# A gated recurrence with a gated convolution behind it: inputs loaded in pieces of 128 tokens, small weights on another queue, four gate tiles in flight

## The chip, the cores and the metric

The kernel runs on one core of a Trainium2 chip. A core has five engines that work side by side and wait for one another through semaphores: TensorE (PE in the profile, its weight loads PEld), VectorE (DVE), ScalarE (ACT), GpSimd (POOL) and SyncE (SP), which here only issues transfers. Sixteen DMA engines move data between HBM and the core's memory. The metric is the device time of one execution in microseconds, the median of several runs.

## The reference

The inputs are `x`, `r_gate` and `i_gate`, each 4 x 6336 x 256 in float32, 25,344 tokens of 256 features in all. Cut to what matters:

```python
log_a = 8.0 * sigmoid(r_gate) * np.log(np.clip(sigmoid(a_param), 1e-6, 1 - 1e-6))
a_t   = np.exp(log_a)
x_g   = np.sqrt(np.maximum(1 - a_t * a_t, 1e-6)) * sigmoid(i_gate) * x
for t in range(S):
    h = a_t[:, t] * h + x_g[:, t]          # a recurrence along the sequence
    y[:, t] = h
gate = sigmoid(causal_conv(y, conv_w))     # five taps, each feature by itself
out  = (gate * (y @ w_val)) @ w_out        # both 256 x 256
```

Every input element is read once and every output element written once: 104 MB with the output.

## The kernel before

**Tiles.** The tokens are cut into 51 tiles `g`, 48 of 512 tokens and three of 256, and these into 28 chunks `c`, mostly of two tiles (`CHUNKS`). Loading, the gates and the output work by tile; the recurrence works by chunk and by half `h` of the 256 features; the square root works by unit, a group of one to three chunks (`UNITS`), because ScalarE needs another function table for it than for exp and tanh.

**One tile's way.** `load` brings `r` and `i` into a buffer `ri` (`NIN` = 3 of them); `r` puts four consecutive tokens on each partition (L248), `i` puts token j x 128 + p on partition p (L249). `loadx` brings `x` in the same way as `i` (L255, `NX` = 5 buffers). `tanh` (L343, ScalarE) makes both gates' tanh in one instruction. `u2` forms (tanh + 1) * x, on VectorE in one instruction (L350) or on GpSimd in two (L353 and L354); the string `U2` says which for each tile. `srT` turns the r half with TensorE so that features lie on partitions (L327), `exp` makes a (L366, ScalarE), `e` squares it (L374, GpSimd), `sq` takes the root (L378, ScalarE, by unit), `nT` turns that back (L387) and `xg` multiplies it into `u` (L394, VectorE). `xT` turns `u` (L327), `scan` runs the recurrence (L415, VectorE), `conv` does the five taps as matmuls with diagonal weights (L441), `tg` is the gate's tanh (L449, ScalarE), `val` and `out` are the two products (L457, L479), `gv` joins gate and value (L467, VectorE), `osb` moves the result out of PSUM (VectorE at L490 or ScalarE at L492, by the string `OSB`), and `store` writes a tile (L497, `NOSB` = 3 buffers).

**Order.** All of it is written out by a planner. `make_jobs` lists each operation's engine, an assumed cost from `COST` and what it depends on; the buffer counts are such dependencies, for instance a load of tile g on the tanh of tile g - `NIN`:

```python
job("load", "DMA", f, [("tanh", g - NIN)])
```

`make_plan` then simulates the engines greedily, the earliest start first and `PRIO` where starts tie, and the kernel emits the operations in the order of the planned starts. Each engine runs its instructions in that order, whatever the chip's real times are. So another cost, priority or string moves instructions on all engines. Every load and store is issued by SyncE, in order: an issue that waits holds back all transfers behind it. The framework gives the transfers eight completion semaphores in turn, so that a transfer also waits until the one eight places before it has landed.

**Setup.** `ap2` (L260) and `wrow` (L262) are small parameters at the head of SyncE's queue; the first six planned loads follow. ScalarE makes log(sigmoid(`a_param`)) by a tanh (L289) and an Ln (L296). The two matrices are cast on their way by GpSimd's own queue.

Of the kernel before, what the change touches and what calls it, by code (L numbers as in the profile page):

```python
# [9 lines left out]
P = 128  # L10
# [5 lines left out]

CHUNKS = [[256], [512]] + [[512, 512]] * 23 + [[512], [256], [256]]

UNITS = [2, 2, 1, 3, 3, 3, 3, 3, 2, 2, 1, 3]
NS = 10  # L20
NE = 8
NU = 10
NY = 6
NIN = 3
NX = 5
NTR = 3
NTI = 6
# [2 lines left out]
BANKS = 4  # L30
PB = dict(srT=2, nT=2, xT=2, ops=2)

OSB = ("DDDDDDDDDADDDDDDDDDDDADDADDDDDDDDADDDADDDDDADADADDDDDDDDDDADADDDDDDAAADDADDDAADADAAADADDAA"
       "AAAADDAAA")

U2 = "PDPDDDDPPPPDDDPPDPPDPPPPPPPPPPPPPPPPDPPPPPPPPPDPPPP"

COST = dict(load=(0.1, 2.7), loadx=(0.05, 1.45), tanh=(0.2, 1.7), u2P=(0.25, 3.15), u2D=(0.15, 1.07), srT=(0.05, 0.45), exp=(0.35, 0.86), e=(0.1, 1.8),
            sq=(0.3, 1.71), nT=(0.05, 0.47), xg=(0.1, 0.58), xT=(0.05, 0.45), scan=(0.21, 2.14), conv=(0.2, 1.1), tg=(0.19, 0.83),
            val=(0.02, 0.93), gv=(0.15, 1.07), out=(0.02, 0.47), osbD=(0.68, 0), osbA=(0.59, 0),  # L40
            store=(0.1, 1.2))
PRIO = dict(load=-0.26, loadx=5.59, store=-2, tanh=6, exp=3.87, sq=5.27, tg=-0.62, srT=-2, nT=2.67, xT=-2,
            conv=4.33, val=-0.49, out=3.64, e=4.3, u2=5.81, xg=1.63, scan=5.49, gv=3.24, osb=-2)
TABLE, SEM, DMA_LAT = 1.3, 0.15, 2.2
FP32 = mybir.dt.float32
BF16 = mybir.dt.bfloat16
ACT = mybir.ActivationFunctionType
ALU = mybir.AluOpType


class Shape:
# [3 lines left out]
    def __init__(self, total, seq):  # L55
# [15 lines left out]
        self.runs, self.npos, batch_of = [], [], []  # L71
        for u, n in enumerate(UNITS):
            runs = []
# [35 lines left out]
def make_jobs(sh):  # L109

    jobs = {op: [] for op in PRIO}
    unit_of = [u for u, n in enumerate(UNITS) for _ in range(n)]
    ends = [sum(UNITS[:u + 1]) for u in range(len(UNITS))]
    qlast = [max(q for q, (w, _) in enumerate(sh.pieces) if w == g) for g in range(len(sh.tiles))]

    def job(op, eng, f, deps, cost=None, bank=0):
        fix, per = COST[cost or op]
        jobs[op].append((eng, fix + per * f, [d for d in deps if d[1] >= 0], bank))  # L120

    for g, (_, n) in enumerate(sh.tiles):
        f = n / WIN
        c = sh.chunk_of[g]
        job("load", "DMA", f, [("tanh", g - NIN)])
        job("loadx", "DMA", f, [("u2", g - NX)])
        job("tanh", "ACT", f, [("load", g), ("u2", g - NTI)]
            + ([("srT", 2 * sh.chunk_of[g - NTR] + 1)] if g >= NTR else []))
        job("u2", "DVE" if U2[g] == "D" else "POOL", f, [("tanh", g), ("loadx", g)] + ([("xT", 2 * sh.chunk_of[g - NU] + 1)] if g >= NU else []), "u2" + U2[g])
        job("nT", "PE", f, [("sq", unit_of[c]), ("xg", g - PB["nT"])], None, 1)  # L130
# [18 lines left out]
    for q, (g, i) in enumerate(sh.pieces):  # L149
        job("out", "PE", 1, [("gv", g), ("osb", q - PB["ops"])], None, 1)  # L150
        job("osb", "DVE" if OSB[q] == "D" else "ACT", 1, [("out", q), ("store", g - NOSB)], "osb" + OSB[q])
    for u, n in enumerate(UNITS):
        size = sum(sh.chunks[c][1] for c in range(ends[u] - n, ends[u])) / CHUNK
        fix, per = COST["sq"]
        jobs["sq"].append(("ACT", fix * len(sh.runs[u]) + per * size, [("e", 2 * ends[u] - 1)], 0))
# [3 lines left out]
def make_plan(sh):  # L159

    jobs = make_jobs(sh)
    reads = dict(exp="srT", xg="nT", scan="xT", osb="out")
    nxt = dict.fromkeys(jobs, 0)
    done, free, order, mode = {}, {}, [], "E"
    bank_free, banks = [0.0] * BANKS, {}
    while True:
        best = None
        for op, todo in jobs.items():  # L170
            i = nxt[op]
            if i == len(todo):
                continue
            eng, dur, deps, need = todo[i]
            t = free.get(eng, 0.0)
            if need:
                b = min(bank_free)
                if b == math.inf:
                    continue
                if b:  # L180
                    t = max(t, b + SEM)
            for d in deps:
                e = done.get(d)
                if e is None:
                    break
                if e + SEM > t:
                    t = e + SEM
            else:
                if best is None or (t, PRIO[op]) < best[:2]:
                    best = (t, PRIO[op], op, i, eng, dur, need)  # L190
        if best is None:
            break
        t, _, op, i, eng, dur, need = best
        if eng == "ACT" and op != "osb":
            if (op == "sq") != (mode == "S"):
                dur += TABLE
            mode = "S" if op == "sq" else "E"
        free[eng] = t + dur
        done[op, i] = t + dur + (DMA_LAT if eng == "DMA" else 0.0)
        if need:  # L200
            banks[op, i] = bank_free.index(min(bank_free))
            bank_free[banks[op, i]] = math.inf
        if op in reads:
            bank_free[banks[reads[op], i]] = t + dur
        order.append((t, op, i, eng, dur))
        nxt[op] += 1
    assert all(nxt[op] == len(todo) for op, todo in jobs.items()), nxt
    order.sort(key=lambda o: o[0])
    return order, banks
# [3 lines left out]
def kernel(  # L213
# [11 lines left out]
    nc = tc.nc  # L225
    B, S, D = x.shape
    assert D == 2 * P, f"kernel assumes D == 256, got {D}"
    H = D // P

    xf = x.rearrange("b s d -> (b s) d")  # L230
    rf = r_gate.rearrange("b s d -> (b s) d")
    if_ = i_gate.rearrange("b s d -> (b s) d")
# [6 lines left out]
    const = ctx.enter_context(tc.tile_pool(name="const", bufs=1))  # L239
# [3 lines left out]
    def load(g):  # L243
        t0, nt = tiles[g]
        nj = nt // P
        ri = inp.tile([P, 2, SUB, D], FP32, name="ri", tag="ri", bufs=NIN)

        nc.sync.dma_start(ri[:, 0, 0:nj, :], rf[t0:t0 + nt, :].rearrange("(p j) d -> p j d", j=nj))  # L248
        nc.sync.dma_start(ri[:, 1, 0:nj, :], if_[t0:t0 + nt, :].rearrange("(j p) d -> p j d", p=P))  # L249
        live["ri", g] = ri  # L250

    def loadx(g):
        t0, nt = tiles[g]
        xt = inp.tile([P, SUB, D], FP32, name="xt", tag="xt", bufs=NX)
        nc.sync.dma_start(xt[:, 0:nt // P, :], xf[t0:t0 + nt, :].rearrange("(j p) d -> p j d", p=P))  # L255
        live["xt", g] = xt

    with tc.manual_schedule():
        ap2 = const.tile([H, P], FP32, name="ap2")
        nc.sync.dma_start(ap2[:], a_param.rearrange("(h p) -> h p", p=P))  # L260
        wrow = const.tile([CONV_K, D], FP32, name="wrow")
        nc.sync.dma_start(wrow[:], moe_conv_w[:, :])  # L262
        before = [(op, g) for _, op, g, eng, _ in plan if eng == "DMA"][:6]
        for op, g in before:
            (load if op == "load" else loadx)(g)

        ident_f = const.tile([P, P], FP32, name="ident_f")
        make_identity(nc, ident_f[:])
# [16 lines left out]
        with tc.tile_pool(name="ps_setup", bufs=1, space=bass.MemoryType.PSUM) as ps_setup:  # L285
            kps = ps_setup.tile([P, H], FP32, name="kps")
            nc.tensor.transpose(out=kps[:], in_=ap2[0:H, :], identity=ident_f[0:H, 0:H])
            kt = const.tile([P, H], FP32, name="kt")
            nc.scalar.activation(out=kt[:], in_=kps[:], func=ACT.Tanh, scale=0.5)  # L289
            ksig = const.tile([P, H], FP32, name="ksig")  # L290
            nc.vector.tensor_scalar(out=ksig[:], in0=kt[:], scalar1=0.5, scalar2=0.5,
                                    op0=ALU.mult, op1=ALU.add)
            nc.vector.tensor_scalar(out=ksig[:], in0=ksig[:], scalar1=1e-6, scalar2=1.0 - 1e-6,
                                    op0=ALU.max, op1=ALU.min)
            kln = const.tile([P, H], FP32, name="kln")
            nc.scalar.activation(out=kln[:], in_=ksig[:], func=ACT.Ln)  # L296
            nc.vector.tensor_scalar(out=khf[:], in0=kln[:], scalar1=0.5 * C_SCALE, scalar2=None, op0=ALU.mult)
            wc_ps = ps_setup.tile([P, H, CONV_K], FP32, name="wc_ps")
            for h in range(H):
                nc.tensor.transpose(out=wc_ps[:, h, :], in_=wrow[0:CONV_K, h * P:(h + 1) * P],  # L300
                                    identity=ident_f[0:CONV_K, 0:CONV_K])
            nc.vector.tensor_copy(out=wcol[:], in_=wc_ps[:])
        diag = const.tile([P, H, CONV_K, P], BF16, name="diag")
        for h in range(H):
            for kk in range(CONV_K):
                nc.vector.tensor_scalar(out=diag[:, h, kk, :], in0=ident_f[:], scalar1=wcol[:, h, kk:kk + 1],
                                        scalar2=None, op0=ALU.mult)
# [186 lines left out]
        def op_store(g, eng):  # L494
# [6 lines left out]
                           nT=op_nT, xg=op_xg, xT=op_xT, scan=op_scan, conv=op_conv, tg=op_tg, val=op_val, gv=op_gv,  # L501
                           out=op_out, osb=op_osb, store=op_store)
# [32 lines left out]
```

## Time and profile before

| | |
|---|---|
| time, median of 3 runs (lowest to highest) | 323.8 us (321.44 to 326.42) |
| span of the profiled run | 324.1 us |
| busy: ScalarE | 289.5 us, 89% |
| busy: VectorE | 270.2 us, 83% |
| busy: TensorE, its weight loads | 246.5 us, 76%; 161.6 us, 50% |
| busy: GpSimd | 236.1 us, 73% |
| moved by DMA | 104.56 MB, mean 323 GB/s |
| packets of SyncE's queue | 67,022, 90.1% of 16 engines' span |
| granted TensorE clock, mean | 0.967 |

Busy time counts instructions that compute; waits, semaphore instructions and the issuing of transfers are not in it. A table by stage gives for each stretch of the span its length and, engine by engine, the busy microseconds with the number of instructions, then the TensorE clock, the DMA engines' busy share and the rate. The share can pass 1 because an engine's packets overlap. A line of waits reads: who waited for whom, microseconds in total, number of waits, the longest. A line of a transfer's issues reads: kind, count, size of one, median microseconds from issue to landing.

### The profile page before, as it was taken

To read this page: it belongs to the slowest core of one execution; us is meant where nothing else is said; L and a number is where in the kernel's file an instruction comes from. 1 tells how busy PE (TensorE), PEld (TensorE's weight loads), DVE (VectorE), ACT (ScalarE), POOL (GpSimd) and SP (SyncE) were. 2 spreads that over 40 slices of the span, in tenths; PEclk is the share of its full clock that TensorE was granted. 3 is DMA by queue.
4 is the path that set the end of the run, shared out by engine and by line. 5 is a ranking of instruction groups with operands and counts; after the bars stand their busy time and mean duration, and the time that the engine had idled before them with its cause. 6 is when DMAs were issued, how large, how long until landed. Compare 5 with 4: busy or idle time off the path is not lost.

```text
span 324.1 us, 7354 instructions
## 1 busy us (share of the span) xinstructions
PE 246.5 (76%) x2987; PEld 161.6 (50%) x2987; DVE 270.2 (83%) x265; ACT 289.5 (89%) x230; POOL 236.1 (73%) x146
## 2 busy tenths in 40 slices
PE   1148426796687787797988778797779896989994
PEld 0044325454455455564654465464546654655653
DVE  3126649999899699999999679988987997999993
ACT  6898899899886899999998999799969999899953
POOL 6427552999899759996599999999995790299200
PEclk9999769999999799999999999999989997999999
DMA  7999999999999999999999999999999984323344
GB/s 217 349 363 375 330 338 357 363 316 389 342 368 385 381 306 342 355 389 400 381 337 404 392 381 310 401 387 395 374 389 377 344 280 169 131 101 161 131 197 194
DMA packets 68432, 104.56 MB, mean 323 GB/s; under 512 B 4391, under 2 KB 55342, under 8 KB 68398
## 3 DMA queue, kind: packets, MB, share of 16 engines
q1 hardware_dynamic: 67022, 103.83, 90.1%
q0 software_dynamic: 1376, 0.26, 0.9%
q8 instruction: 23, 0.38, 0.5%
q14 instruction: 11, 0.09, 0.1%
HBM read 78.39 MB, written 25.95 MB: 322 GB/s over the span
## 4 chain that ended last, share of the span: by engine, by line
ACT 20%; DVE 18%; PE 18%; DMA 17%; issue 14%; POOL 10%; SPq 2%; ACTq 0%; DVEq 0%; POOLq 0%
DMA ri<-in_i_gate_dram 10%; DVE yring L415 9%; DMA xt<-in_x_dram 7%; ACT tring L343 6%; PE bank L479 5%; ACT ering L378 4%; POOL ering L374 4%; PE gp L441 4%; POOL uring L354 4%; PE val L457 3%; ACT tg L449 3%; PE bank L327 3%; DVE gv L467 3%; DVE osb L490 3%; DVE uring L394 3%
## 5 line engine op out<-in xcount | busy, mean ns | idle before, releaser
L374 POOL TENSOR_TENSOR ering<-aring 128x1024 f32<-128x1024 f32 (+2 forms) x56 | 97.5, 1765 | 44.6 <-ACT aring L366 36.5
L415 DVE TENSOR_TENSOR_SCAN yring<-aring,yring,bank 128x1024 bf16<-128x1024 f32 (+5 forms) x54 | 109.4, 2046 | 0.4 <-PE bank L327 0.4
L354 POOL TENSOR_TENSOR uring<-t,xt 128x1024 bf16<-128x1024 f32 (+1 forms) x39 | 89.9, 2304 | 18.2 <-DMA xt<-in_x_dram 9.1
L343 ACT ACTIVATE tring<-ri 128x2048 bf16<-128x2048 f32 (+1 forms) x51 | 93.9, 1865 | 10.0 <-DMA ri<-in_i_gate_dram 9.6
L441 PE MATMUL gp<-yring,diag 64*64 64x512 bf16 (+16 forms) x1196 | 68.2, 351 | 8.6 <-ACT tg L449 6.4
L479 PE MATMUL bank<-wo,gv 128*128 128x256 bf16 x396 | 58.1, 279 | 10.5 <-DVE gv L467 3.7
L467 DVE SCALAR_TENSOR_TENSOR gv<-tg,val 128x1024 bf16<-128x1024 bf16 (+1 forms) x54 | 60.3, 1120 | 6.7 <-PE val L457 4.3
L366 ACT ACTIVATE aring<-bank,khf 128x1024 f32<-128x1024 bf16 (+2 forms) x56 | 59.4, 1109 | 6.2 <-PE bank L327 5.6
L449 ACT ACTIVATE tg<-gp 128x1024 bf16<-128x1024 f32 (+1 forms) x51 | 51.1, 1002 | 6.5 <-PE gp L441 6.4
L457 PE MATMUL val<-yring,wv 128*128 128x512 bf16 (+1 forms) x204 | 52.8, 383 | 4.1 <-DVE gv L467 3.9
L490 DVE COPY osb<-bank 128x512 f32<-128x512 f32 x69 | 45.6, 679 | 8.6 <-PE bank L479 7.4
L479 PEld LDWEIGHTS <-gv 128*128 128x128 bf16 x396 | 36.7, 99 | 29.4 <-issue 14.6
L378 ACT ACTIVATE ering<-ering,b 128x2048 bf16<-128x2048 f32 (+3 forms) x15 | 46.7, 3112 | 2.3 <-POOL ering L374 1.9
L441 PEld LDWEIGHTS <-diag 64*64 64x64 bf16 x1196 | 31.6, 108 | 32.6 <-issue 17.4
L387 PE MATMUL bank<-ident_b,ering 128*128 128x128 bf16 x396 | 30.7, 231 | 22.2 <-ACT ering L378 19.8
L353 POOL TENSOR_SCALAR t<-tring 128x1024 f32<-128x1024 bf16 (+1 forms) x39 | 45.0, 1154 | 2.0
L394 DVE TENSOR_TENSOR uring<-bank,uring 128x1024 bf16<-128x1024 bf16 (+1 forms) x51 | 33.0, 666 | 15.9 <-PE bank L387 9.6
L327 PE MATMUL bank<-ident_b,tring 128*128 128x128 bf16 x396 | 32.1, 232 | 17.3 <-ACT tring L343 12.5
L387 PEld LDWEIGHTS <-ering 128*128 128x128 bf16 x396 | 26.0, 104 | 27.9 <-ACT ering L378 22.8
L327 PEld LDWEIGHTS <-tring 128*128 128x128 bf16 x396 | 26.0, 104 | 25.9 <-ACT tring L343 14.2
L327 PE MATMUL bank<-ident_b,uring 128*128 128x128 bf16 x396 | 31.9, 224 | 8.9 <-DVE uring L394 6.0
L327 PEld LDWEIGHTS <-uring 128*128 128x128 bf16 x396 | 25.4, 101 | 17.4 <-DVE uring L394 8.0
(31 smaller groups left out, 109.2 us busy)
## 6 DMA issues: line engine op xcount, KB each, us to landing
ri<-in_r_gate_dram SPq DMA_DIRECT2D x48, 512.0 KB, 7.0
ri<-in_i_gate_dram SPq DMA_DIRECT2D x48, 512.0 KB, 7.9
xt<-in_x_dram SPq DMA_DIRECT2D x48, 512.0 KB, 8.0
out_dram<-osb SPq DMA_DIRECT2D x48, 512.0 KB, 4.9
ri<-in_r_gate_dram SPq DMA_DIRECT2D x3, 256.0 KB, 3.2
ri<-in_i_gate_dram SPq DMA_DIRECT2D x3, 256.0 KB, 3.4
xt<-in_x_dram SPq DMA_DIRECT2D x3, 256.0 KB, 7.5
out_dram<-osb SPq DMA_DIRECT2D x3, 256.0 KB, 2.0
```

Of the source, the lines that this page charges most:

```text
L327: nc.tensor.transpose(out=dst[:, col:col + P], in_=src[:, j, h * P:(h + 1) * P], identity=ident_b[:])
L343: nc.scalar.activation(out=tring[:, r:i + 1:i - r, 0:nj, :], in_=ri[:, :, 0:nj, :], func=ACT.Tanh, scale=0.5)
L354: nc.gpsimd.tensor_tensor(out=u, in0=t1, in1=xt, op=ALU.mult)
L366: nc.scalar.activation(out=aring[:, h, a0:a0 + nt].rearrange("c (w p j) -> c w p j", p=P, j=nj), in_=live.pop(("srT", k))[:, 0:nt].rearran ...
L374: nc.gpsimd.tensor_tensor(out=ering[:, h, e0:e0 + nt], in0=a, in1=a, op=ALU.mult)
L378: nc.scalar.activation(out=nring[:, :, 2 * e0:2 * e0 + m], in_=ering[:, :, e0:e0 + m], func=ACT.Sqrt, scale=-0.25, bias=b025[:, 0:1])
L415: nc.vector.tensor_tensor_scan(out=yring[:, h, y0 + c0:y0 + c1], data0=aring[:, h, a0 + c0:a0 + c1], data1=xT[:, c0:c1], initial=0.0 if fr ...
L441: nc.tensor.matmul(out=gp[64 * h:64 * h + 64, m, c0:c1], lhsT=diag[rows, h, kk, rows], rhs=yring[rows, h, src:src + c1 - c0], start=(sh == 0),
L449: nc.scalar.activation(out=tg[:, :, 0:nt], in_=live.pop(("gp", g))[:, :, 0:nt], func=ACT.Tanh, scale=0.5)
L457: nc.tensor.matmul(out=val[:, m, 0:nt], lhsT=wv[:, hk, m * P:(m + 1) * P], rhs=yring[:, hk, y0:y0 + nt], start=(hk == 0), stop=(hk == H - 1))
L467: nc.vector.scalar_tensor_tensor(out=gv[:, 0:nj, hs, :].rearrange("c j h p -> c j (h p)"), in0=tg[:, hs, 0:nt].rearrange("c h (p j) -> c j ...
L479: nc.tensor.matmul(out=ops[:, e * D:(e + 1) * D], lhsT=gv[:, 2 * i + e, hk, :], rhs=wo[:, hk, :], start=(hk == 0), stop=(hk == H - 1))
```

## The change

It has four parts. First, the loads of `i` and `x` are split: one transfer per 128 tokens instead of one per tile. Such a transfer reads 128 rows of 1 KB that lie in a row in HBM, one to each partition[...]. Second, the two small parameters go on ScalarE's queue, and ScalarE's start uses exp and Ln, which share a function table, with the tanh table loaded by an instruction of its own that waits for nothing. Third, four instead of three buffers for the gates. Fourth, the planner starts DMA and ScalarE at a later planned time (`START`, `ACT_START`), costs `u2` on VectorE higher, and has new priorities, units and strings: 13 units for 12; `u2` on VectorE for 7 tiles for 12; `osb` on VectorE for 69 pieces as before, in other places.

```diff
-UNITS = [2, 2, 1, 3, 3, 3, 3, 3, 2, 2, 1, 3]
+UNITS = [1, 1, 2, 1, 2, 4, 3, 3, 3, 3, 1, 2, 2]
-NIN = 3
+NIN = 4
-U2 = "PDPDDDDPPPPDDDPPDPPDPPPPPPPPPPPPPPPPDPPPPPPPPPDPPPP"
+U2 = "DPPPDPPPPPDDPPPDDPPPPPPPPPPPPPPPPPPPPPPDPPPPPPPPPPP"
...
-PRIO = dict(load=-0.26, loadx=5.59, store=-2, tanh=6, exp=3.87, sq=5.27, tg=-0.62, srT=-2, nT=2.67, xT=-2,
-            conv=4.33, val=-0.49, out=3.64, e=4.3, u2=5.81, xg=1.63, scan=5.49, gv=3.24, osb=-2)
+PRIO = dict(load=3.81, loadx=4.34, store=2.61, tanh=1.36, exp=-1.22, sq=0.49, tg=-1.74, srT=-1.43, nT=0.13,
+            xT=2.16, conv=3.97, val=0.26, out=1.67, e=4.3, u2=6, xg=-2, scan=4.12, gv=-1.47, osb=-2)
+START, ACT_START = 0.9, 4.6
...
-    done, free, order, mode = {}, {}, [], "E"
+    done, free, order, mode = {}, dict(DMA=START, ACT=ACT_START), [], "E"
...
-        nc.sync.dma_start(ri[:, 1, 0:nj, :], if_[t0:t0 + nt, :].rearrange("(j p) d -> p j d", p=P))
+        for j in range(nj):
+            nc.sync.dma_start(ri[:, 1, j, :], if_[t0 + j * P:t0 + (j + 1) * P, :])
...
-        nc.sync.dma_start(xt[:, 0:nt // P, :], xf[t0:t0 + nt, :].rearrange("(j p) d -> p j d", p=P))
+        for j in range(nt // P):
+            nc.sync.dma_start(xt[:, j, :], xf[t0 + j * P:t0 + (j + 1) * P, :])
...
-        nc.sync.dma_start(ap2[:], a_param.rearrange("(h p) -> h p", p=P))
+        nc.scalar.dma_start(ap2[:], a_param.rearrange("(h p) -> h p", p=P))
-        nc.sync.dma_start(wrow[:], moe_conv_w[:, :])
+        nc.scalar.dma_start(wrow[:], moe_conv_w[:, :])
+        nc.scalar.preload_act_table_set("natural_log_exp_and_others")
...
-            nc.scalar.activation(out=kt[:], in_=kps[:], func=ACT.Tanh, scale=0.5)
+            nc.scalar.activation(out=kexp[:], in_=kps[:], func=ACT.Exp, scale=-1.0)
-            nc.vector.tensor_scalar(out=ksig[:], in0=kt[:], scalar1=0.5, scalar2=0.5,
-                                    op0=ALU.mult, op1=ALU.add)
+            nc.vector.tensor_scalar(out=ksig[:], in0=kexp[:], scalar1=1.0, scalar2=None, op0=ALU.add)
+            nc.vector.reciprocal(out=ksig[:], in_=ksig[:])
...
             nc.scalar.activation(out=kln[:], in_=ksig[:], func=ACT.Ln)
+            nc.scalar.preload_act_table(ACT.Tanh)
```

More of the change, by code (lines that the diff above doesn't have):

```diff
@@ L31 @@
 PB = dict(srT=2, nT=2, xT=2, ops=2)
-OSB = ("DDDDDDDDDADDDDDDDDDDDADDADDDDDDDDADDDADDDDDADADADDDDDDDDDDADADDDDDDAAADDADDDAADADAAADADDAA"
+OSB = ("DDDDDDDDDDDDDDADDDDDDDDADDDDDDDDDDDDDDDDDDDDDDDDDADDDAAADAADADDDDDAAADADAADADDDAAAADAAADDD"
        "AAAADDAAA")
-U2 = "PDPDDDDPPPPDDDPPDPPDPPPPPPPPPPPPPPPPDPPPPPPPPPDPPPP"
-COST = dict(load=(0.1, 2.7), loadx=(0.05, 1.45), tanh=(0.2, 1.7), u2P=(0.25, 3.15), u2D=(0.15, 1.07), srT=(0.05, 0.45), exp=(0.35, 0.86), e=(0.1, 1.8),
+U2 = "DPPPDPPPPPDDPPPDDPPPPPPPPPPPPPPPPPPPPPPDPPPPPPPPPPP"
+COST = dict(load=(0.1, 2.7), loadx=(0.05, 1.45), tanh=(0.2, 1.7), u2P=(0.25, 3.15), u2D=(0.2, 1.55), srT=(0.05, 0.45), exp=(0.35, 0.86), e=(0.1, 1.8),
             sq=(0.3, 1.71), nT=(0.05, 0.47), xg=(0.1, 0.58), xT=(0.05, 0.45), scan=(0.21, 2.14), conv=(0.2, 1.1), tg=(0.19, 0.83),
@@ L287 @@
             nc.tensor.transpose(out=kps[:], in_=ap2[0:H, :], identity=ident_f[0:H, 0:H])
-            kt = const.tile([P, H], FP32, name="kt")
-            nc.scalar.activation(out=kt[:], in_=kps[:], func=ACT.Tanh, scale=0.5)
+            kexp = const.tile([P, H], FP32, name="kexp")
+            nc.scalar.activation(out=kexp[:], in_=kps[:], func=ACT.Exp, scale=-1.0)
             ksig = const.tile([P, H], FP32, name="ksig")
-            nc.vector.tensor_scalar(out=ksig[:], in0=kt[:], scalar1=0.5, scalar2=0.5,
-                                    op0=ALU.mult, op1=ALU.add)
+            nc.vector.tensor_scalar(out=ksig[:], in0=kexp[:], scalar1=1.0, scalar2=None, op0=ALU.add)
+            nc.vector.reciprocal(out=ksig[:], in_=ksig[:])
             nc.vector.tensor_scalar(out=ksig[:], in0=ksig[:], scalar1=1e-6, scalar2=1.0 - 1e-6,
```

## The prediction

> **What bounds the kernel now.** I read the table of stages first (busy time of each engine in each stretch of the span, then TensorE clock, DMA share, GB/s), because the page's mean shares (ScalarE 89%, VectorE 83%, DMA about 90%) mix a start, a stream and a drain.
>
> ```profile
> 0.00:10.00 10.00, 1.22 (x7) 0.81 (x7) 3.22 (x16) 6.53 (x9) 6.16 (x14) 1.00 0.86 237
> 10.00:20.00 10.00, 2.46 (x20) 1.97 (x20) 1.11 (x1) 9.24 (x8) 2.67 (x3) 1.00 1.11 362
> 80.00:120.00 40.00, 30.95 (x381) 20.14 (x382) 35.69 (x35) 33.93 (x26) 32.92 (x17) 0.96 1.01 357
> 200.00:240.00 40.00, 32.01 (x384) 20.96 (x381) 37.37 (x34) 35.74 (x27) 38.25 (x22) 1.00 1.06 384
> 280.00:300.00 20.00, 18.37 (x236) 11.02 (x235) 20.00 (x15) 19.09 (x24) 17.90 (x14) 1.00 0.29 115
> 300.00:324.00 24.00, 20.04 (x240) 12.40 (x236) 18.21 (x24) 15.31 (x19) 1.62 (x3) 0.98 0.44 176
> ```
>
> After PE and its weight loads come VectorE, ScalarE, GpSimd. From 10 to about 260 us the DMA engines are full (share 1.01 to 1.11, 352 to 384 GB/s, 367 as the mean of 40 to 240 us) and ScalarE is about 92% busy; from 280 us there are only stores, and VectorE and ScalarE are full. So two resources stand level: the queue of transfers, and ScalarE with 289.5 us of work. ScalarE idles 34.6 us in all: 3.5 before 10 us, 8.7 after 300 us, some 22 between. The waits say for what:
>
> ```profile
> ACT tring L343 <- DMA ri<-in_i_gate_dram: 9.6, 9, 2.2
> POOL uring L354 <- DMA xt<-in_x_dram: 9.1, 4, 4.3
> ACT tg L449 <- PE gp L441: 6.4, 9, 1.3
> DVE uring L350 <- DMA xt<-in_x_dram: 6.2, 4, 2.6
> ACT aring L366 <- PE bank L327: 5.6, 7, 1.3
> ```
>
> (total, times, longest). ScalarE waits for gate tiles 9.6 us, the largest entry that more gate buffers can touch; x makes GpSimd and VectorE wait 15.3 us. Then the queue of SyncE, its own waits and issues (min/median/max ns of one issue):
>
> ```profile
> SPq L497 <- DVE osb L490: 91.6, 38, 5.7
> SPq L248 <- ACT tring L343: 48.6, 27, 4.1
> ```
> ```profile
> L248 SPq DMA_DIRECT2D ri<-in_r_gate_dram x51: 327/341/1124, 1.5 to 277.0; - x51
> L249 SPq DMA_DIRECT2D ri<-in_i_gate_dram x51: 417/434/1511, 1.9 to 277.4; - x51
> ```
> ```profile
> ri<-in_i_gate_dram SPq DMA_DIRECT2D x48, 512.0 KB, 7.9
> out_dram<-osb SPq DMA_DIRECT2D x3, 256.0 KB, 2.0
> ```
>
> SyncE spends most of its time waiting for buffers, yet the DMA stays full: a 512 KB load lands 7.9 us after its issue, so a long backlog covers waits of up to 5.7 us. Last, ScalarE's start:
>
> ```profile
> 3.92 0.20 ACT L296 ACTIVATE kln<-ksig 128x2 f32<-128x2 f32 x1
> 5.14 1.28 ACT L343 ACT_TABLE_LOAD   x1 [1.02 <-DMA ri<-in_i_gate_dram]
> 6.43 1.06 ACT L343 ACTIVATE tring<-ri 128x1024 bf16<-128x1024 f32 x1
> ```
>
> The table load stands behind the wait for the first gates, so its 1.28 us lie on the path.
>
> **What the Trainium skill says.** (1) "ScalarE: Activation LUTs", What ACT_TABLE_LOAD costs: a load takes about 1283 ns and a drain about as much again. The trace has 1283 ns, but the activation behind starts within 0.02 us, so I count 1.28 us. (2) "DMA: Bandwidth & Descriptors", Rules for kernel authors: transfers are to be joined, under 64 KB is mostly overhead; the new pieces are 128 KB, above that, and nothing here shows their price. (3) Same page, Latency and other measured facts: rows at a pitch that is a large power of two slow HBM, measured from 512 KiB pitch up. Before, each partition of i and x reads rows 128 KB apart. The trace shows no such loss: its packet records have medians of 46 ns for 1,024 B, 84 for 2,048 and 159 for 4,096, one straight line of 8.3 ns plus 27.2 GB/s, though only the first kind has the pitch. (4) Same page, Issuing engines are not separate DMA queues: transfers of other queues share the same 16 engines, so moving weights saves only issue time.
>
> **The change, part by part.**
>
> *Reading in a row.* Packets stay 1 KB, since each row of the tile is still 1 KB. What order can win is the excess over the median: 50,693 packets have a mean of 49.5 ns, so 3.5 x 50,693 / 16 = 11.1 us of each engine. But 4 KB packets have an excess of 5.4% too (167.6 over 159) against 7.5%; the 2.1% more is 46 x 0.021 x 50,693 / 16 = 3 us. Both ends: 0 and 11 us; I take 3.
>
> *More transfers.* 498 on SyncE instead of 206. Each ends with 16 completion packets of 4 B, mean 9.5 ns: 292 x 9.5 ns = 2.8 us more per engine. This cancels the 3.
>
> *Issuing.* Before: 51 x (0.341 + 0.434 + 0.506 + 0.344) = 83 us. One 128-row issue is not shown for 1 KB rows; 128 rows of 4 KB take 0.341, four times as many rows 0.434 to 0.506. With the 0.05 us between issues, 0.39 each (at most 0.56): 498 x 0.39 = 194 us (at most 277). A full tile needs 10 issues, 3.9 us, for 2 MB that take 2.097 / 367 = 5.7 us. It lies beside the data. In runs of small pieces alone it does not: 131 KB per 0.39 us is 335 GB/s; the stores and r loads of 512 KB between make it up.
>
> *Window.* In both programs a transfer waits for the one eight places before it. That was 8 x 509 KB = 4.1 MB, 11 us of data; it becomes 1.7 MB on average (4.5 us), 1.05 MB (2.9 us) in runs of small pieces. A 256 KB store lands in 2.0 us, of which 0.7 is data, so 1.3 us is fixed; eight pieces of 131 KB in 1.3 + 0.4 us would allow over 600 GB/s. So it doesn't limit unless landing under load costs 2.9 us. Behind a SyncE wait for `osb` all later loads queue. SyncE now comes to that wait some 6 us later relative to the data, when `osb` (wait at most 5.7 us) is mostly ready; so the wait shrinks with the backlog. Cost 0 to 18 us (second rival); I take 1.
>
> *Four gate tiles.* L248 waited 48.6 us for the tanh that frees a buffer; a fourth one lets gates run one tile (5.7 us) further ahead. ScalarE's 9.6 us on gates has longest waits of 2.2, so most could go; x then comes later in the same full stream. I take -4 us.
>
> *Start.* Two issues of weights (0.36 + 0.27 and gaps, 0.74 us) leave ahead of the first gates; exp and ln share a table, and the tanh table is loaded before the gates arrive. ScalarE: two issues to 1.4, table to 2.7, exp, three VectorE steps of about 0.3 us, ln at 3.9, table to 5.2, tanh at 5.2 instead of 6.43: -1.2 us. It has work queued behind, so this carries on.
>
> *The new plan.* ScalarE: 26 table loads for 25, 17 square roots for 15 over the same data (fixed part 0.3 us, from 2.00 and 3.71 us for 2048 and 4096): +1.9 us. Evictions stay 69 and 30. VectorE: u2 on 7 tiles instead of 12, -5 x 1.94 and one of half size, -10.5 us. GpSimd: 5 more tiles at 1.20 + 2.39 and one half tile less, +19.6 us, 256 in all. VectorE is full only after 280 us, where both plans give u2 to GpSimd, so its gain counts little: -1. GpSimd, 38.25 of 40 busy at 200 to 240 us, has slack before 120 us, where four of the five moved tiles lie; +0. More semaphores per instruction: GpSimd's gap between its two u2 steps is 0.08 us with two, three or four waits alike, so 0.
>
> Sum: 0 + 1 - 4 - 1.2 + 1.9 - 1 = -3.3; the reorder's remaining gain, of the 12 us of ScalarE waits on PE, a sixth, -2: -5.3, so 323.8 - 5.3 = **318.5 us**.
>
> **Rivals.** *The stream speeds up:* the 11 us of excess go and ScalarE no longer waits for data. Then ScalarE's floor: 291.4 of work + 2.5 idle at the start + 8.7 at the end + 6 for PE = 309. For: DMA full for 250 us. Against: the straight line of packet times. *The stream starves (slower):* short window and issue rate pull it to 340 GB/s. The 88 MB of 20 to 260 us (367 x 240) then take 258 us, +18; with 4 won elsewhere: 338. For: 335 GB/s in runs, backlog a quarter. Against: 3.9 us of issue in 5.7. *GpSimd becomes the bound:* its 19.6 us more, half in its full stretch: 324 + 10 - 4 = 330. Against: 256 us in some 290. *The gains and costs cancel:* 324.
>
> **Numbers.** Forecast 0.45, faster stream 0.18, cancel 0.15, starving 0.16, GpSimd 0.06. Within 2% is 317.3 to 330.3: forecast has two fifths of its weight below, giving faster 0.18 + 0.18 = 0.36; slower takes 0.16 and most of 0.06, 0.21; same 0.43. Range 307 to 335: it holds the faster stream's centre and stops short of full starving.
>
> **What would show it.** Right: first tanh at about 5.2 us; 1 KB packets still about 46 ns; GB/s of 355 to 375 from 20 to 240 us; SyncE's waits for `osb` far below 91.6 us; ScalarE's wait on gates under 6 us. Wrong: issues of 0.5 us or more, GB/s at or under 340 and DMA share under 0.95 in the stream (starving); 1 KB packets shorter or 390 GB/s and more (faster stream); GpSimd without idle and others waiting for `uring`.

## The result and the profile after

The changed kernel takes 356.95 us (355.08 to 360.48, 4 runs) against 325.11 us of the kernel before on the same chip: ratio 1.105, 95% interval 1.090 to 1.119. The forecast was 318.5 us, its range ended at 335. Times here are of all runs and ratios of the fast ones alone; the profiled run, the longest of the four, counts as slow, but the fast one of e3 below has the same rates (299, 311 and 324 GB/s from 40, 120 and 200 us).

Read in the order of the prediction, first the table of stages (PE, weight loads, VectorE, ScalarE, GpSimd, then TensorE clock, DMA share, GB/s):

```profile
80.00:120.00 40.00, 30.05 (x291) 19.47 (x288) 30.54 (x28) 33.05 (x23) 25.21 (x15) 0.83 0.97 331
120.00:160.00 40.00, 28.46 (x332) 20.43 (x331) 28.83 (x29) 31.70 (x22) 29.07 (x17) 0.83 0.93 311
...
200.00:240.00 40.00, 28.70 (x350) 18.70 (x348) 29.14 (x30) 28.54 (x21) 29.58 (x18) 0.87 0.95 318
...
280.00:300.00 20.00, 15.75 (x192) 10.34 (x190) 15.99 (x19) 16.94 (x14) 18.27 (x11) 1.00 0.86 302
```

The stream has slowed and become longer. From 40 to 240 us it moves 313 GB/s (the mean of five stretches) where the kernel before moved 367, the DMA engines are no longer full, and from 80 to 120 and 200 to 240 us, which the prediction shows for the kernel before, every computing engine is less busy than it was. The stretch from 280 us, which held little but stores before (115 GB/s), still carries loads at 302; the last piece of x is issued at 310 us. At 313 GB/s the 73.4 MB of those 200 us at 367 take some 35 us longer, as much as the whole loss of 32.

The waits say who went short:

```profile
POOL uring L360 <- DMA xt<-in_x_dram: 39.6, 7, 12.7
DVE uring L356 <- DMA xt<-in_x_dram: 29.5, 4, 12.5
...
DVE uring L400 <- POOL uring L360: 23.8, 10, 8.1
...
ACT tring L349 <- DMA ri<-in_i_gate_dram: 13.2, 7, 5.1
```

Waits for input came to 24.9 us before (9.6 for gates, 15.3 for x); now it is 82.3, most of it for x. Then SyncE, the queue that starts all of it:

```profile
SPq L251 <- DMA ri<-in_r_gate_dram: 23.4, 27, 1.8
SPq L503 <- DVE osb L496: 23.1, 11, 4.7
SPq L503 <- ACT osb L498: 21.7, 8, 6.8
SPq L258 <- DMA ri<-in_r_gate_dram: 12.3, 14, 1.4
...
SPq L249 <- ACT tring L349: 2.9, 3, 2.2
```

The prediction shows the wait before for the `osb` that VectorE makes, 91.6 us. ScalarE makes some of it too:

```profile
SPq L497 <- ACT osb L492: 32.9, 15, 7.3
```

So before, SyncE waited 124.5 us for `osb` and 48.6 for the tanh that frees a gate buffer: it was ahead of everybody. Now these are 44.8 (23.1 and 21.7) and 2.9. In their place its issues of loads wait 48.7 us, the sum of ten such lines, for an earlier transfer to land, where it was 4.8. No data dependence asks for that: it is the window, the wait for the transfer eight places before. The trace holds the landing for 368 such pairs: no issue ends before that landing, and 142 start within 0.3 us after it (before: 3 of 148). SyncE has fallen behind. Its issues (min/median/max ns), and sizes with median microseconds to landing:

```profile
L251 SPq DMA_DIRECT2D ri<-in_i_gate_dram x198: 327/430/1358, 1.2 to 302.6; - x198
```
```profile
L258 SPq DMA_DIRECT2D xt<-in_x_dram x198: 327/430/1499, 21.4 to 310.2; - x198
```
```profile
ri<-in_i_gate_dram SPq DMA_DIRECT2D x198, 128.0 KB, 5.0
xt<-in_x_dram SPq DMA_DIRECT2D x198, 128.0 KB, 3.6
```

An issue takes 0.430 us and the gap behind it 0.044, so 0.474 us, where I had priced 0.39. A piece of 128 KB lands in 3.6 to 5.0 us, where I had thought 1.7. Both limits can be seen in one stretch of SyncE's time line, a run of 20 pieces of x:

```profile
48.82 0.37 SPq L503 DMA_DIRECT2D out_dram<-osb  x1
49.23 10.06 SPq L258 DMA_DIRECT2D xt<-in_x_dram  x20
```

One piece of 131 KB in 0.503 us is 261 GB/s. Most of the pieces here stand 0.474 us apart, so at SyncE's own rate (276 GB/s); eight in flight with a landing of 3.6 us would allow 1.05 MB / 3.6 us = 292 GB/s. Two limits so close together can't be told apart from this trace alone. The experiments had to do it, as far as they could.

### The profile page after: what moved, and what is told of

Its sections match the earlier page's. It is cut to its first block, busy times and chain, and to the rows that moved or that the text cites. A ratio compares the mean times of both kernels' runs of the same rounds, so it can differ in the third digit from the quotient of the medians.

```text
span 358.7 us, 7805 instructions
## 1 busy us (share of the span) xinstructions
PE 262.4 (73%) x2987; PEld 173.3 (48%) x2987; DVE 257.1 (72%) x261; ACT 292.5 (82%) x233; POOL 245.9 (69%) x156
## 3 DMA queue, kind: packets, MB, share of 16 engines
q1 hardware_dynamic: 71712, 103.84, 85.6%
## 4 chain that ended last, share of the span: by engine, by line
DMA 35%; DVE 14%; PE 11%; issue 10%; SPq 10%; ACT 10%; POOL 9%; DVEq 0%; POOLq 0%; ACTq 0%
DMA ri<-in_i_gate_dram 15%; DMA ri<-in_r_gate_dram 13%; DVE yring L421 6%; DMA xt<-in_x_dram 6%; POOL uring L360 5%; SPq L258 5%; SPq L251 3%; PE gp L447 3%; DVE gv L473 3%; PE bank L485 3%; DVE osb L496 3%; POOL ering L380 3%; ACT tring L349 2%; PE bank L333 2%; ACT tg L455 2%
## 5 line engine op out<-in xcount | busy, mean ns | idle before, releaser
L360 POOL TENSOR_TENSOR uring<-t,xt 128x1024 bf16<-128x1024 f32 (+1 forms) x44 | 102.5, 2330 | 55.9 <-DMA xt<-in_x_dram 39.6
L380 POOL TENSOR_TENSOR ering<-aring 128x1024 f32<-128x1024 f32 (+2 forms) x56 | 94.6, 1716 | 24.3 <-ACT aring L372 16.1
L349 ACT ACTIVATE tring<-ri 128x2048 bf16<-128x2048 f32 (+1 forms) x51 | 93.4, 1858 | 13.7 <-DMA ri<-in_i_gate_dram 13.2
L447 PE MATMUL gp<-yring,diag 64*64 64x512 bf16 (+14 forms) x1196 | 72.5, 373 | 3.1 <-ACT tg L455 1.3
L393 PE MATMUL bank<-ident_b,ering 128*128 128x128 bf16 x396 | 33.4, 245 | 29.0 <-ACT ering L384 18.3
L333 PE MATMUL bank<-ident_b,tring 128*128 128x128 bf16 x396 | 36.5, 252 | 22.4 <-ACT tring L349 16.0
L496 DVE COPY osb<-bank 128x512 f32<-128x512 f32 x69 | 44.8, 679 | 11.0 <-PE bank L485 6.3
L384 ACT ACTIVATE ering<-ering,b 128x4096 bf16<-128x4096 f32 (+4 forms) x17 | 47.3, 2780 | 1.4 <-POOL ering L380 1.0
L393 PEld LDWEIGHTS <-ering 128*128 128x128 bf16 x396 | 28.9, 111 | 34.9 <-ACT ering L384 20.4
L333 PEld LDWEIGHTS <-tring 128*128 128x128 bf16 x396 | 30.3, 114 | 31.5 <-ACT tring L349 17.5
L333 PE MATMUL bank<-ident_b,uring 128*128 128x128 bf16 x396 | 34.0, 236 | 12.8 <-DVE uring L400 12.0
L333 PEld LDWEIGHTS <-uring 128*128 128x128 bf16 x396 | 28.2, 107 | 19.9 <-issue 12.4
```

Of the source, the lines that this page charges most:

```text
L333: nc.tensor.transpose(out=dst[:, col:col + P], in_=src[:, j, h * P:(h + 1) * P], identity=ident_b[:])
L349: nc.scalar.activation(out=tring[:, r:i + 1:i - r, 0:nj, :], in_=ri[:, :, 0:nj, :], func=ACT.Tanh, scale=0.5)
L360: nc.gpsimd.tensor_tensor(out=u, in0=t1, in1=xt, op=ALU.mult)
L380: nc.gpsimd.tensor_tensor(out=ering[:, h, e0:e0 + nt], in0=a, in1=a, op=ALU.mult)
L393: nc.tensor.transpose(out=nT[:, j, h * P:(h + 1) * P], in_=nring[:, h, n0 + j * P:n0 + (j + 1) * P], identity=ident_b[:])
L447: nc.tensor.matmul(out=gp[64 * h:64 * h + 64, m, c0:c1], lhsT=diag[rows, h, kk, rows], rhs=yring[rows, h, src:src + c1 - c0], start=(sh == 0),
```

## The experiments

The theory from these lines: the split loses the time, because eight transfers now hold a quarter to two fifths of the bytes, and the DMA engines run short of queued work (**window**). Its rivals: SyncE's issue time by itself (**issue**), the new order of rows in HBM (**rows**), a price that each transfer has on the DMA engines (**price**), and the other parts of the change (**plan, start, gate tiles**). Ratios are to the kernel before on the same chip, with 95% intervals.

| label | edit | median us | ratio |
|---|---|---|---|
| e1 | changed kernel, i and x joined again | 326.25 | 1.005 [1.003, 1.008] |
| e2 | kernel before, split alone | 361.28 | 1.112 [1.105, 1.120] |
| e3 | changed kernel, rows of a piece not adjacent | 359.31 | 1.105 [1.096, 1.114] |
| e4 | changed kernel, pieces of 256 tokens | 325.78 | 1.008 [1.004, 1.011] |
| e5 | e1 with six tiny transfers per full tile | 381.39 | 1.164 [1.155, 1.173] |
| e6 | e1 with 18 counts on SyncE per tile | 326.41 | 1.012 [1.008, 1.016] |
| e7 | the same with 40 | 327.48 | 1.011 [1.008, 1.014] |
| e13 | the same with 48 | 329.40 | 1.018 [1.011, 1.025] |
| e11 | the same with 60 | 343.69 | 1.059 [1.053, 1.066] |
| e10 | e1 with a window of 2 places | 437.25 | 1.348 [1.341, 1.356] |
| e9 | the same with 3 | 378.02 | 1.166 [1.158, 1.174] |
| e14 | the same with 4 | 336.99 | 1.042 [1.034, 1.050] |
| e16 | e4 with 32 counts on SyncE per tile | 325.63 | 1.011 [1.000, 1.021] |
| e18 | e4 with a window of 4 places | 378.07 | 1.174 [1.165, 1.184] |
| e17 | the same with 5 | 346.24 | 1.074 [1.063, 1.086] |
| e8 | kernel before, i and x in 4 KB packets | 321.58 | 0.990 [0.982, 0.998] |
| e12 | kernel before, start part alone | 323.97 | 0.996 [0.993, 0.999] |
| e15 | e12 with four gate tiles | 331.69 | 1.025 [1.019, 1.031] |

### Which part: e1 and e2

```diff
-        for j in range(nj):
-            nc.sync.dma_start(ri[:, 1, j, :], if_[t0 + j * P:t0 + (j + 1) * P, :])
+        nc.sync.dma_start(ri[:, 1, 0:nj, :], if_[t0:t0 + nt, :].rearrange("(j p) d -> p j d", p=P))
```

e1 does this to the changed kernel, and the same to x. e2 puts only the split into the kernel before.

> The changed kernel with i and x loaded by one transfer per tile again; plan, start and four gate tiles stay. Theory 1 (SyncE's queue: an issue costs 0.47 us back to back, and 10 of them per tile, with the waits between, starve the DMA engines): the loss goes with the split, 314 to 323 us, DMA share 1.0 or more in the stream, SyncE issuing about 105 us instead of 232. Theory 2 (the new plan loses: more u2 on GpSimd, x loaded late): 345 us or more, GpSimd and VectorE still waiting some 60 us for x.

> The kernel before with i and x loaded in pieces of 128 tokens, nothing else changed. Theory 1 (SyncE's queue): 345 to 365 us, 280 to 330 GB/s in the stream, waits for x and i of GpSimd, VectorE and ScalarE together over 60 us. Theory 2 (the plan): 320 to 328 us.

Joined, all other parts of the change together are worth +0.5%, so they cost a little where e1's expectation had them gain; the split alone costs 11.2%. In e1 the stream is whole again, and SyncE waits for buffers as it did before the change:

```profile
120.00:160.00 40.00, 34.80 (x451) 23.52 (x450) 35.32 (x32) 38.04 (x28) 39.07 (x23) 0.93 1.06 375
```
```profile
SPq L501 <- DVE osb L494: 104.2, 41, 6.9
SPq L249 <- ACT tring L347: 46.4, 27, 5.0
```

In e2 the input goes missing at once, here more at the gates than in the changed kernel (42.6 us against 13.2); its plan is the old one:

```profile
ACT tring L345 <- DMA ri<-in_i_gate_dram: 42.6, 12, 7.4
POOL uring L356 <- DMA xt<-in_x_dram: 36.5, 7, 10.0
```

So the split is the cause, whatever stands around it.

### Neither the rows nor a price of each transfer: e3 and e8

e3 keeps the split, but piece j takes the tokens j, j + 4, j + 8 and so on of its tile, so that rows of a piece lie 4 KB apart. It thus computes with i and x in another order of tokens than the reference.

```diff
+        rows = if_[t0:t0 + nt, :].rearrange("(p j) d -> j p d", j=nj)
         for j in range(nj):
-            nc.sync.dma_start(ri[:, 1, j, :], if_[t0 + j * P:t0 + (j + 1) * P, :])
+            nc.sync.dma_start(ri[:, 1, j, :], rows[j])
```

> The changed kernel, same number and size of transfers, but each piece takes every fourth token of the tile[...]. It computes on i and x in another token order than r, so its output is not the reference's; the work is the same. If reading in a row is worth nothing: 352 to 362 us, 1 KB packets of 46 ns at the median as before. If it had been worth the 11 us that the excess of the 1 KB packets allowed: 362 to 370 us and a mean of 1 KB packets above 55 ns.

1.105 and 1.105: the order of rows has no part in it. The packet records agree: 1 KB packets have a median of 46 ns and a mean of 50.5 in e3, 46 and 50.6 in the changed kernel, 46 and 49.5 in the kernel before. Taking the rows of a piece from one stretch of HBM gained nothing.

e8 puts four consecutive tokens of i and x on a partition, as for r, in the kernel before (again another order of tokens): all packets are 4 KB.

```diff
-        nc.sync.dma_start(ri[:, 1, 0:nj, :], if_[t0:t0 + nt, :].rearrange("(j p) d -> p j d", p=P))
+        nc.sync.dma_start(ri[:, 1, 0:nj, :], if_[t0:t0 + nt, :].rearrange("(p j) d -> p j d", j=nj))
```

> The kernel before with i and x laid out like r, four consecutive tokens to a partition, so that all packets are of 4 KB; nothing else changed. i and x then are in another token order than the recurrence, so the output is not the reference's; the work is the same. Packets need 159 ns for 4 KB instead of 4 x 46, some 20 us less of each DMA engine. If the stream of transfers bounds the kernel before: 308 to 318 us. If ScalarE and the planned order do: 320 to 326 us.

It is 1.0% faster, though it relieves each DMA engine of some 18 us of packets (85.3% of 321.7 us against 90.1% of 324.1). The kernel before is thus not bound by the stream alone; other work stands level with it.

A price of each transfer on the DMA engines can be read from the packets too. The 294 transfers that the changed kernel has more than e1 add 4,704 packets of 4 B, 2.6 us of each engine. All packets of SyncE's queue take 307 us of each engine there (85.6% of 358.7), 292 in the kernel before. But this rises with a narrow window alone: e9, described below, has the transfers of e1 with three of them in flight. The queue in e1, then in e9 (packets, MB, share of a span of 323.2 and 374.1 us):

```profile
q1 hardware_dynamic: 67008, 103.82, 90.8%
```
```profile
q1 hardware_dynamic: 67008, 103.82, 83.8%
```

That is 293 us and 313 us for the same packets. So little of the loss is a price of the number of transfers.

### Issue time: e6, e7, e13, e11, e4 and e5

e4 makes two pieces of 256 tokens, so 300 SyncE issues (its expectation counts six too many) rather than 498 or 204, and room for 2.8 MB in flight. It keeps half of the split and loses nothing:

> The changed kernel with i and x in two pieces of 256 tokens per tile: 306 transfers in place of 498. Theory 1: 306 x 0.47 = 145 us of issue, 2.9 us per tile of 5.7 us of data, so nearly all of the loss is gone, 318 to 328 us. A price that grows in proportion to the number of transfers would put it at a third of the way from the joined to the changed kernel, some 330 us. Theory 2: as the changed kernel, 345 us or more.

e5 adds transfers that move 4 B to each partition, to have the number of issues and of places in the window without the data:

```diff
+    def tiny(n):
+        for _ in range(n):
+            t = inp.tile([P, 8], FP32, name="tiny", tag="tiny", bufs=12)
+            nc.sync.dma_start(t[:, 0:1], if_[0:P, 0:1])
```

> The changed kernel with joined loads (326.3 us) and, behind each load of i and of x, three more transfers of 128 words of 4 B into a scratch tile (one for a half tile). So SyncE has 498 issues and every transfer waits for the one eight places before it, as with the split, but the data still come in 512 KB pieces. Number of transfers is the cause, by issue time or by the window of eight: 348 to 362 us. The small pieces of data themselves (128 KB landing one by one) are the cause: 326 to 333 us.

It came out worse than the split itself and than both its expectations, at 381 us, and decides nothing: 294 such transfers are 37,632 packets, and the packets take 37 us more of each DMA engine than in e1 (88.2% of 375.0 us), so it isn't the one suspect alone.

The cleaner way to take SyncE's time is an instruction that only counts a semaphore up, of which there are N behind each i and each x load of the joined kernel; in the trace they stand 0.059 us apart.

```diff
+    def delay():
+        for _ in range(N):
+            nc.sync.value_load(word[0:1, 0:1])
```

(The loaded value is not used, and what is left of it on SyncE is the count.) N is 9, 20, 24 and 30.

> The changed kernel with joined loads and, behind each load of i and of x, nine instructions on SyncE that only count up a semaphore which nobody waits for: 18 per tile, estimated at 0.07 us each, 1.3 us of SyncE's time per tile, no transfer and no place in the window. Issue time alone is the cause: some of the loss, 327 to 336 us. The window of eight is the cause: 324 to 328 us.

> As the one with nine, with twenty: 40 per tile, about 2.8 us of SyncE's time per tile, as much as the six additional issues of the split at 0.47 us. Issue time alone is the cause: 345 to 360 us. The window of eight (a transfer waits for the one eight places before it, which with small pieces is little data) is the cause: 324 to 330 us. Both by half: 335 to 345 us.

> The changed kernel with i and x joined again and 24 bare semaphore counts on SyncE behind each i and x load: 48 per tile at the 0.059 us measured in e7 are 2.83 us of SyncE per tile, which is what the split adds (6 more issues at 0.474 us are 2.84 us). The data, the number of transfers and what each moves are those of e1. Between 2.36 us per tile (327.5 us, e7) and 3.5 us per tile (343.7 us, e11) lies an edge. If SyncE's own time is a part of the split's loss: 331 to 336 us. If the window of eight transfers is nearly all of it: 326 to 330 us. If SyncE's time is the whole of it: 350 us or more.

> As the one with twenty, with thirty semaphore counts behind each load of i and x: 60 per tile at the 0.059 us that the run with twenty showed, 3.5 us of SyncE's time per tile, more than the six additional issues of the split (2.8 us). If SyncE's time is no cause: 327 to 333 us. If there is an edge that twenty (2.4 us) did not reach: 340 us or more.

Per tile that takes 1.1, 2.4, 2.8 and 3.5 us of SyncE, and costs 0.2, 1.2, 3.2 and 17.4 us over e1; these runs were on other chips than e1, and by the ratios it is 2, 2, 4 and 17. The split adds six issues of 0.474 us, 2.84 per tile: the amount of e13 (e7 was meant to reach it and stayed below). So with room for 4.1 MB in flight, SyncE's issue time makes 3 or 4 of the split's 31 us (357.0 less 326.3), and an edge comes right behind it.

### The window: e10, e9, e14

The joined kernel again, with each transfer held until the load k places before has landed:

```diff
+    def room(word):
+        if len(sent) >= k and sent[-k] is not None:
+            nc.sync.value_load(sent[-k].bitcast(mybir.dt.int32))
+        sent.append(word)
...
+        room(xt[0:1, 0, 0:1])
         nc.sync.dma_start(xt[:, 0:nt // P, :], xf[t0:t0 + nt, :].rearrange("(j p) d -> p j d", p=P))
```

(Each load has such a line. A store takes a place but is not waited for, so the window is a little wider than k.)

Few issues, large transfers, and little room for bytes in flight: the mean transfer is 103.8 MB / 204 = 0.51 MB, so 1.02, 1.53 and 2.04 MB against 4.1.

> The same with two places, 1 MB in flight, what the split has where eight small pieces follow one another. Window is the cause: 375 us or more, below 280 GB/s. A price of each transfer: 326 to 335 us.

> The changed kernel with joined loads; each transfer additionally waits until the one three places before it has landed, if that was a load. Number and size of transfers stay at 204 and 512 KB, but at most three, 1.5 MB, are in flight instead of eight; the split has eight of 208 KB on average, 1.7 MB. Window is the cause of the split's loss: 345 to 365 us, 290 to 335 GB/s in the stream. A price that each transfer has on the DMA engines is the cause: 326 to 331 us.

> The changed kernel with i and x joined, each transfer held until the load four places before it has landed, so at most 2.1 MB of loads are in flight. With three places (1.57 MB) the time was 378 us and the middle of the stream ran at 303 GB/s; with the eight of the joined kernel 326 us and 375 GB/s. If the rate follows bytes in flight over a landing of about 6 us: 330 to 350 GB/s in the middle and 335 to 352 us. If three places lost for another reason than the bytes (the order of the waits on SyncE's queue), four lose nearly as much: 360 to 375 us.

437, 378 and 337 us; e9 lost more than the 345 to 365 us that were expected of it. The landings of x in e10, e9 and e14, in this order:

```profile
DMA to landing us min/median/max: 2.8/4.3/6.5
```
```profile
DMA to landing us min/median/max: 3.9/5.2/7.3
```
```profile
DMA to landing us min/median/max: 4.6/6.1/7.6
```

Bytes in flight over the landing give the rate: 1.02 / 4.3 = 237 GB/s, 1.53 / 5.2 = 294, 2.04 / 6.1 = 334; measured from 40 to 240 us are 246, 302 and 349 (means of five stretches). The three landings lie on a line, 2.5 us plus 1.76 us per MB in flight. The Trainium skill ("DMA: Bandwidth & Descriptors", Anatomy of one DMA) has such a form, some 2.0 us fixed plus the bytes at 436 GB/s, for GpSimd's kind of queue and for the bytes of one transfer; the fixed part here, an estimate from the line, is 2.5 us with other transfers around, and not the 1.3 I took.

### Which of the two in the changed kernel: e16, e17, e18

One doubt was left. With a narrow window SyncE's issue time can't be hidden by a backlog, so it might still be the main cause in the changed kernel, where runs of pieces were issued back to back. e16 takes the pieces of 256 tokens and has 8 counts behind each: SyncE needs 0.412 + 8 x 0.059 = 0.88 us for 256 tokens of x, near the 0.95 of the split, but 2.8 MB are in flight. e17 and e18 take the same pieces with no such counts and a window of 5 and 4 places: 1.73 and 1.38 MB, on both sides of the split's 1.67 (103.8 MB / 498 x 8), with less issue time.

> The kernel of e4 (i and x in two pieces of 256 tokens per tile) with 8 bare semaphore counts on SyncE behind each piece: 32 per tile at 0.059 us are 1.9 us, so that SyncE needs 0.95 us for 256 tokens, the same as for two pieces of 128 in the changed kernel. The window of eight transfers still holds 2.8 MB on average, 2.1 MB in runs of x pieces, against 1.67 and 1.05 MB. If the narrow window is the main cause of the split's loss: 327 to 335 us. If SyncE's rate of issue in runs (131 KB per 0.474 us, 276 GB/s) is the main cause whatever is in flight: 345 to 360 us. Between these both have a part.

> The kernel of e4 with each load held until the load five places before it has landed: 1.75 MB in flight on average, 1.31 MB in runs of x pieces, and 198 issues fewer on SyncE than in the changed kernel. If the bytes in flight alone make the loss: 345 to 365 us (e9 with 1.57 MB had 378, e14 with 2.1 MB 337). If the loss needs the issue time as well: 330 to 340 us.

> The same with four places: 1.40 MB on average and 1.05 MB in runs of x pieces, as small as the changed kernel's in runs and smaller on average. If the bytes in flight set the rate: 370 to 400 us, so over the changed kernel's 357. If the issue time is the main cause: 335 to 350 us.

e16 loses nothing that can be seen (325.6 us, e4 325.8; at least 327 had been expected). Its SyncE time stays a little under the split's; e13, which reaches it, lost 3 or 4 us. e17 loses 20 us and e18 52, both within what was expected of the window. One stretch of e16, e17 and e18, in this order:

```profile
120.00:160.00 40.00, 34.69 (x451) 23.58 (x456) 36.22 (x33) 38.86 (x30) 38.98 (x24) 0.96 1.04 367
```
```profile
120.00:160.00 40.00, 32.02 (x399) 23.91 (x400) 34.88 (x35) 35.39 (x25) 35.51 (x21) 0.86 0.99 322
```
```profile
120.00:160.00 40.00, 25.05 (x255) 19.34 (x257) 21.78 (x24) 27.90 (x19) 23.82 (x14) 0.70 0.92 299
```

As means of 40 to 240 us these are 363, 335 and 295 GB/s. With nearly the changed kernel's rate of issue and a wide window the DMA stays full; with windows on both sides of its own and fewer issues, the rates lie on both sides of its 313. All runs in order of the window's mean room: 1.02 MB 437 us, 1.38 MB 378, 1.53 MB 378, **the changed kernel 1.67 MB 357**, 1.73 MB 346, 2.04 MB 337, 2.8 MB 326, 4.1 MB 326. The changed kernel lies on that row.

This is room, not what stands in it. What stands there is the rate times the landing, an estimate from the medians of the four kinds of transfer between 40 and 240 us: 1.4 MB in e18 and 1.7 in e17, whose windows are thus full, 2.8 in e1 of its 4.1, and 1.5 in the changed kernel of its 1.67, nearly full. A straight line between e18 and e17 gives the changed kernel 352 us by room, which would leave 5 us for its issue time, and 369 by what stands in it, which would leave none. That division stays open. The opposite trial, pieces of 128 KB with more than eight places, was not run.

### The start and the gate tiles: e12 and e15

e12 is the kernel before with only the start part (small weights on ScalarE's queue, Exp and Ln in one table, tables loaded early); e15 adds `NIN = 4` to it. The planner reads `NIN`, so e15 also has another order of work.

> The kernel before with the change's start alone: small weights on ScalarE's queue, exp and Ln from one table, the tanh table loaded without waiting. First tanh at 5.2 instead of 6.4 us. If ScalarE's start carries through: 1 us faster, a ratio of 0.995 to 0.998. If the stream of transfers or the order takes it back: 1.000.

> The kernel before with the earlier start (weights on ScalarE's queue, one table for Exp and Ln) and four input tiles in flight in place of three, the split left out. The start alone was 0.996 of before. If the fourth tile helps: 0.98 to 0.99. If the bound stands elsewhere: 0.99 to 1.01.

The start alone gains 0.4%, [0.1, 0.7], about the 1.2 us of the prediction, and the first tanh begins at 5.31 us:

```profile
5.31 1.06 ACT L345 ACTIVATE tring<-ri 128x1024 bf16<-128x1024 f32 x1
```

The fourth gate tile, with the order that goes with it, costs 7.7 us, 331.7 against 324.0, and e15 is slower than both its expectations allow. Waits in e12, then e15:

```profile
POOL uring L356 <- DMA xt<-in_x_dram: 14.1, 3, 6.2
...
ACT tring L345 <- DMA ri<-in_i_gate_dram: 10.6, 9, 2.1
```
```profile
POOL uring L356 <- DMA xt<-in_x_dram: 27.0, 5, 10.2
...
ACT tring L345 <- DMA ri<-in_i_gate_dram: 1.8, 1, 1.8
```

The wait it was meant for has gone, 10.6 to 1.8 us, and GpSimd's wait for x has grown by 12.9. That would fit a full stream, where what comes earlier for one input makes the other later, but how much of the 7.7 us is that, and how much the other order, was not tried.

## Why the prediction was wrong

**The step that failed** is the window: "So it doesn't limit unless landing under load costs 2.9 us", priced at 1 us with a range to 18. Its condition was the right one and the size was wrong. Landing under load costs 3.6 us (x) and 5.0 us (i), so the split cost 31 us rather than 1, of which some 5 may be issue time. The 1.7 us of the prediction were a fixed 1.3 and the data of one piece. By the line of e10, e9 and e14 the fixed part is 2.5 us, and the 1.05 MB in flight add 1.8: 4.3 us, an estimate from 512 KB loads. The 1.3 us came from a 256 KB store of 2.0 us, the median of three, two of which are the last of the drain, where little else is in flight. The trace of before had the warning: the third, issued at 29 us in the full stream, landed in 4.4 us. And the 7.9 us of the 512 KB loads I read wholly as backlog. Landing and bytes in flight are one question: 4.1 MB over 7.9 us is 520 GB/s, enough; a quarter of the bytes would have to land in a quarter of the time.

**The rival that happened** was "the stream starves", with a chance of 0.16. Two of its three signs came, GB/s under 340 (313) and a DMA share under 0.95 (0.94 as a mean, 0.92 to 0.97); issues of 0.5 us did not. It was too small, 338 us, as it took 340 GB/s for the rate, and gave a credit of 4 us for the other parts that did not come.

**Issuing** was priced at 0.39 us and measured 0.474. The 0.341 us of the r load was that of an issue which mostly follows a wait (327 ns is the fastest in both programs); in a row an issue takes 430. "It lies beside the data" holds where the window is wide: 0 us in e16, 3 or 4 in e13. Whether it still holds in the changed kernel is the division left open above. SyncE's waits for `osb` shrank as foreseen, but to 44.8 us from 124.5: the prediction read the 91.6 for VectorE's part alone, and the longest wait was 7.3 us, not 5.7.

**Reading in a row**, 3 us (0 to 11): 0. The packets are unchanged. For the high end, the excess of the mean over the median had been taken as something that order could win; it is there with every order.

**Size of a transfer**: the Trainium skill ("DMA: Bandwidth & Descriptors", Rules for kernel authors) puts the border of "mostly overhead" at 64 KB. Here 256 KB pieces cost nothing and 128 KB pieces 10%, and 512 KB loads with a window of two places 35%. What decided here is the bytes that are in flight together, not the size of one.

**Start**, -1.2 us: right alone (e12). In the changed kernel the first tanh came at 5.96, not 5.2, since it then waited 0.66 us for a piece of i.

**Four gate tiles**, -4 us: with joined loads the wait went as said (1.8 us in e15, 2.4 in e1; 13.2 in the changed kernel), the gain did not come (e15, +7.7 us with the order that goes with it).

**The new plan**: ScalarE 292.5 us of work (291.4 expected), VectorE 257.1 (259.7), GpSimd 245.9 (256, too high; the sum there is right, but of six full tiles less a half one, not of five). In e1 GpSimd is full in three of the five stretches from 40 to 240 us (39.07 of 40 us from 120 us), before in two, so its work is hardly free. With e15 at +2.5% and e1 at +0.5%, the plan seems to win back some 2%; that is a difference of two runs and was not tried by itself. The credits of 5 us for tiles and plan were wrong by about 8, the lesser error.

## What to carry to other kernels

When a change cuts transfers smaller and something fixes how many may be in flight, work out bytes in flight over landing time, and take the landing from a transfer under full load, with the data of all that are in flight; a rate below what the stream needs is the new bound, even though issuing fits beside the data. A backlog is also what hides SyncE's waits for buffers and its issue time: before taking it away, ask what was leaning on it. A buffer more for one input of a full stream may only move the wait to the next input, as in e15.

## What the runs showed of the hardware

- Landing of a 512 KB load of x under load: 4.3 us with room for 1.02 MB in flight, 5.2 with 1.53, 6.1 with 2.04. A full stream (367 GB/s) needed more room than 2.0 MB (349 GB/s); 2.8 MB were enough.
- An issue on SyncE: 0.430 us and a gap of 0.044 in a row, 0.327 after a pause. A bare semaphore count: 0.059 us.
- 1 KB packets take 46 ns (median) whether the rows of a transfer are 128 adjacent ones in HBM, 128 that lie 4 KB apart, or 512 adjacent rows of which every 128th goes to the same partition. Their mean rises with a narrow window: 49.2 ns in e1, 53.0 in e9.
